# Who forms the lower parts of W_out's blocks in the first MLP of an attention-and-two-MLPs kernel: VectorE instead of GpSimd

## The chip, the cores and the metric

The kernel runs on one core of one Trainium2 chip. The core has a matrix engine (TensorE, PE in the profile; its weight loads are PEld), three engines for elementwise work (VectorE, DVE; ScalarE, ACT; GpSimd, POOL), and a queue that issues the DMAs (SyncE, SP). Each engine takes its instructions strictly in the order of its own queue, and waits on semaphores for the others. The metric is the device time of one execution in microseconds; the median of several executions is compared.

## The reference

```python
attn = causal_softmax(q @ k.T / sqrt(64) + bias(s)) @ v      # 4 batches, 8 heads, 576 positions, 64 wide
x = attn.reshape(2304, 512)
h = x @ w_in1                                                # 512 -> 2048
x = (max(h, 0) + alpha * min(h, 0)) @ w_out1                 # 2048 -> 512
h = x @ w_in2
out = (max(h, 0) ** 2) @ w_out2
```

All of it is wanted to about float32 precision. The four weight matrices arrive as 64-bit floats.

## The kernel before

The program has three stages in a row: attention (to about 217 us), the first MLP (about 217 to 635 us), and the second MLP, which uses a seven-product scheme in place of eight block products (from 635 us). The change lies in the first MLP.

TensorE multiplies in a format with fewer mantissa bits than float32 (fp32r), so every operand is split into a high part (a cast by ScalarE) and a low part (the operand less its high part), and each product is made as three products: high by high, high by low, low by high (TERMS).

The first MLP runs over three thirds of the tokens (c = 0, 1, 2; 768 tokens each) and, in each, over the 16 blocks f of 128 hidden units: 48 steps. A step has these parts:

- split_w(0, f, 0) makes wi_hi (ScalarE, L526) and wi_lo (L528) from a block of W_in, split_w(0, f, 1) makes wo_hi and wo_lo from a block of W_out. Both subtractions stand on L528, for wi on VectorE and for wo on GpSimd. wi has two buffers, wo three.
- mlp_mm (L552): 24 matmuls into two PSUM banks ph, one for each half of the 768 tokens.
- mlp_act: for each half, two VectorE instructions that read ph (L571, L572) form gg; then ScalarE casts gg to the high part of gs (L574) and VectorE subtracts for the low part (L575). L572 also frees its ph bank for the next step's matmuls.
- mlp_out (L673): 24 matmuls of gs and wo into the accumulators po, one step later than mlp_mm.

Beside that, in the gaps, the weights are turned from 64-bit to 32-bit floats. conv does one half of a block: ScalarE scales the two words (L114 into cv_g, L115 into the destination), VectorE forms a mask and shifts (L116, L117, both into cv_t), and GpSimd adds the two as integers (L120). In the first third of the steps the destinations are the blocks wf of the first MLP's own weights, two in a step. From about 338 us on they are blocks wc of the second MLP: there GpSimd also forms sums and differences of blocks (L151 to L154), SP writes the result to DRAM (w1D, from wc), and since wc has one buffer the next L115 waits for that DMA. For W_out of the second MLP the result is split first (whl: L164, L165).

At each change of the third c, the x of the next third is split into xs (L538 on ScalarE, L539 on VectorE).

The order of the instructions on each engine isn't written by hand: the kernel is built with a scheduler that places instructions by its own estimate of their times. A change of engine for one instruction therefore moves others too.

Of the kernel before, what the change touches and what calls it, by code (L numbers as in the profile page):

```python
# [8 lines left out]
F32 = mybir.dt.float32  # L9
# [10 lines left out]
def attention_then_two_mlps(  # L20
# [13 lines left out]
    nc = tc.nc  # L34
# [485 lines left out]
    def split_w(l, f, half):  # L520
        w = wf[l, f]
        nm = ("wi", "wo")[half]
        pool = pools["mp"] if half else pp
        hi = pool.tile([P, 512], F32R, name=nm + "_hi", tag=nm + "_hi", bufs=2 + half)
        lo = pool.tile([P, 512], F32R, name=nm + "_lo", tag=nm + "_lo", bufs=2 + half)
        nc.scalar.copy(hi, w[:, half])  # L526
        eng = nc.vector if half == 0 else nc.gpsimd
        eng.tensor_sub(lo, w[:, half], hi.bitcast(F32))  # L528
        return hi, lo

    W = 2 * HT
# [76 lines left out]
    for g in range(len(units) + LAG + PVLAG):  # L608
# [23 lines left out]
        if live and i == 3:  # L632

            with tc.issue_after(last):
                if cq:
                    w_conv(*cq.pop(0))
                elif n >= NP - 2:
                    first.append(split_w(0, n - NP + 2, 0))
                elif n >= NP - 6:
                    xs.append(make_xk(0, n - NP + 6))  # L640
            if lq:
                w_load(*lq.pop(0))
# [314 lines left out]
    for step, (c, f) in enumerate(steps):  # L957
# [7 lines left out]
        if step > 0 and step + 1 < len(steps):  # L965
            wi = split_w(0, steps[step + 1][1], 0)
        wo = split_w(0, f, 1)
        if step == 0:
            ph = early
# [85 lines left out]
```

## Time and profile before

| | us |
|---|---|
| median of 3 runs | 1009.21 (1007.92 to 1013.36) |
| the profiled execution | 1006.86 |
| its span, first to last instruction | 1005.1 |
| attention | about 217 |
| first MLP | about 418 |
| second MLP | about 370 |

The profile is of one execution. Busy times of an engine say what it did, not what it cost: an engine's idle time matters only where another engine waits for it. TensorE's granted clock was 0.991 of full speed on average, so nearly all matmuls ran at the upper of its two levels.

### The profile page before, as it was taken

How to read it: one execution, taken by the hardware profiler on the slowest of the kernel's cores; microseconds unless marked ns; L12 is line 12 of the kernel's file. 1: busy time of each engine (PE TensorE's matmuls, PEld its weight loads, DVE VectorE, ACT ScalarE, POOL GpSimd, SP SyncE). 2: the span in 40 equal slices, each digit the busy share in tenths (PEclk: the TensorE clock that was granted, in tenths of full speed). 3: DMA queues.
4: the chain of work that ended last, by engine and by line, in shares of the span. 5: the costliest groups of instructions: out<-in, count | busy, mean ns of one | idle time of the engine just before them, and what ended most of it. 6: DMA issues, size and time to landing. Idle time of an engine off the chain costs nothing.

```text
span 1005.1 us, 18047 instructions
## 1 busy us (share of the span) xinstructions
PE 970.0 (97%) x6440; PEld 896.1 (89%) x6440; DVE 810.3 (81%) x1504; ACT 559.7 (56%) x1120; POOL 470.9 (47%) x526
## 2 busy tenths in 40 slices
PE   6899999999999999999999999989999999999998
PEld 5677778778999989989899999889999999999998
DVE  8799889869888898778896777678985889768774
ACT  7798889964444454434544433456453664446442
POOL 7778777645555567675555441234102540034400
PEclk9799999999999999999999999999999999999999
DMA  6666454314434334445373341854677446754274
GB/s 167 167 161 163 119 128 114 73 33 124 127 126 126 104 119 157 158 157 168 125 230 116 116 156 49 323 159 127 221 278 280 125 151 235 267 182 136 90 254 138
DMA packets 105049, 157.05 MB, mean 156 GB/s; under 512 B 31584, under 2 KB 80224, under 8 KB 99584
## 3 DMA queue, kind: packets, MB, share of 16 engines
q1 hardware_dynamic: 104960, 155.91, 49.3%
q8 instruction: 51, 0.84, 0.3%
q14 instruction: 38, 0.31, 0.1%
HBM read 117.00 MB, written 29.88 MB: 146 GB/s over the span
## 4 chain that ended last, share of the span: by engine, by line
PE 56%; DVE 21%; DMA 8%; POOL 7%; ACT 5%; issue 4%; SPq 0%; POOLq 0%; ACTq 0%; DVEq 0%
PE acc L918 15%; PE ph L552 6%; PE po L673 5%; PE b L791 4%; PE a L791 4%; PE c L791 4%; DVE cv_t L117 3%; PE ps_tr L443 3%; DMA w1D<-wc 3%; PE ps_xb L493 2%; DVE gg L571 2%; PE d L791 2%; DVE wi_lo L528 2%; DVE gg L572 2%; PE ps_xa L482 2%
## 5 line engine op out<-in xcount | busy, mean ns | idle before, releaser
L552 PE MATMUL ph<-xs,wi_hi 128*128 128x384 f32 x768 | 199.5, 339 | 7.2 <-DVE gg L572 4.1
L918 PE MATMUL acc<-w2s,th 128*128 128x256 f32 x1512 | 184.7, 283 | 3.3 <-ACT th L707 3.1
L918 PEld LDWEIGHTS acc<-w2s,th 128*128 128x128 f32 x1512 | 183.3, 192 | 4.3 <-ACT th L707 3.5
L673 PE MATMUL po<-gs,wo_hi 128*128 128x512 f32 (+1 forms) x768 | 166.8, 336 | 1.9 <-DVE xT L262 1.4
L552 PEld LDWEIGHTS ph<-xs,wi_hi 128*128 128x128 f32 x768 | 136.7, 189 | 13.8 <-DVE gg L572 6.0
L673 PEld LDWEIGHTS po<-gs,wo_hi 128*128 128x128 f32 x768 | 121.0, 188 | 16.7 <-DVE xT L262 2.1
L552 PE MATMUL ph<-xs,wi_lo 128*128 128x384 f32 x384 | 129.2, 336 | 0.0
L574 ACT CAST gs<-gg 128x768 fp32r<-128x768 f32 (+1 forms) x48 | 39.8, 829 | 139.8 <-DVE gg L572 139.7
L528 POOL TENSOR_TENSOR wo_lo<-wf,wo_hi 128x512 fp32r<-128x512 f32 x48 | 79.9, 1666 | 70.0 <-ACT wo_hi L526 70.0
L707 ACT CAST th<-g 128x768 fp32r<-128x768 f32 x84 | 69.8, 835 | 75.1 <-PE acc L918 57.0
L708 DVE TENSOR_TENSOR th<-g,th 128x768 fp32r<-128x768 f32 x84 | 84.5, 1014 | 23.2 <-ACT th L707 23.2
L673 PE MATMUL po<-gs,wo_lo 128*128 128x256 f32 (+1 forms) x384 | 99.2, 335 | 0.0
L411 POOL TENSOR_SCALAR pr<-pr,rs 128x128 f32<-128x128 f32 (+3 forms) x128 | 73.7, 589 | 42.0 <-DVE rs L408 17.5
L802 POOL TENSOR_TENSOR g<-g 128x384 f32<-128x384 f32 x24 | 21.1, 877 | 154.0 <-ACT g L801 117.1
L708 DVE TENSOR_TENSOR w1h<-w1f,w1h 128x512 fp32r<-128x512 f32 (+1 forms) x96 | 67.9, 720 | 26.5 <-ACT w1h L707 25.8
L575 DVE TENSOR_TENSOR gs<-gg,gs 128x768 fp32r<-128x768 f32 (+1 forms) x48 | 51.8, 1079 | 38.8 <-ACT gs L574 38.8
L398 ACT ACTIVATE pr<-pr,nmax 128x128 f32<-128x128 f32 (+3 forms) x128 | 71.2, 559 | 16.9 <-DVE nmax L386 11.4
L707 ACT CAST w1h<-w1f 128x512 fp32r<-128x512 f32 (+1 forms) x96 | 53.8, 564 | 43.5 <-PE b L791 24.2
L552 PEld LDWEIGHTS ph<-xs,wi_lo 128*128 128x128 f32 x384 | 72.5, 189 | 0.3 <-issue 0.2
L117 DVE SCALAR_TENSOR_TENSOR cv_t<-cv_g,cv_t 128x512 uint32<-128x512 uint32 x64 | 70.8, 1111 | 1.6
L802 POOL TENSOR_TENSOR g<-u 128x384 f32<-128x384 f32 x48 | 49.4, 1030 | 42.4 <-ACT u L801 42.2
L120 POOL TENSOR_TENSOR wc<-cv_t,wc 128x512 uint32<-128x512 uint32 x32 | 43.7, 1373 | 53.5 <-DVE cv_t L117 26.4
(157 smaller groups left out, 2151.9 us busy)
## 6 DMA issues: line engine op xcount, KB each, us to landing
w2s<-w2D SPq DMA_DIRECT2D x42, 1024.0 KB
w1f<-w1D SPq DMA_DIRECT2D x72, 256.0 KB
raw_w<-in_moe_w_in_dram SPq DMA_DIRECT2D x32, 512.0 KB
w2D<-whl SPq DMA_DIRECT2D x16, 896.0 KB
raw_w<-in_moe_w_out_dram SPq DMA_DIRECT2D x24, 512.0 KB
w1D<-wc SPq DMA_DIRECT2D x8, 896.0 KB
QM<-QS SPq DMA_DIRECT2D x15, 288.0 KB
KH<-KS SPq DMA_DIRECT2D x15, 288.0 KB
```

The lines of the kernel that those rows point to most:

```text
L117: nc.vector.scalar_tensor_tensor(t, g.bitcast(U32), 3, t, ALU.logical_shift_left, ALU.bitwise_or)
L398: last = nc.scalar.activation(o, o, AF.Exp, bias=m, scale=-1.0, accum_out=sums[:, h : h + 1])
L411: nc.gpsimd.tensor_scalar(pr[:, :w], pr[:, :w], rs[:, h : h + 1], 1.0, ALU.mult, ALU.mult)
L528: eng.tensor_sub(lo, w[:, half], hi.bitcast(F32))
L552: nc.tensor.matmul(ph[h][:, :HT], ws[a][:, kb * P : (kb + 1) * P], xs[kb][:, bb, h * HT : (h + 1) * HT], start=(cnt == 0), stop=(cnt == 3 ...
L575: sub = nc.vector.tensor_sub(z[:, 1], a, z[:, 0].bitcast(F32))
L673: nc.tensor.matmul(acc, ws[a][:, m * P : (m + 1) * P], gs[:, bb, c_], start=first_ and z == 0, stop=lst and z == 2, skip_group_check=True,)
L707: a = nc.scalar.copy(dst[:, 0], src)
L708: v = nc.vector.tensor_sub(dst[:, 1], src, dst[:, 0].bitcast(F32))
L791: nc.tensor.matmul(pt[:, :HT], hl[:, a, c0 + kb * P : c0 + (kb + 1) * P], xc[i][:, b, kb, :], start=(first and cnt == 0), stop=(cnt == 5), ...
L802: nc.gpsimd.tensor_tensor(dst, r, r, ALU.mult)
L918: nc.tensor.matmul(acc[tb // 2][:, (tb % 2) * 256 : (tb % 2 + 1) * 256], th[:, x, qq, tb * P : (tb + 1) * P], ws[:, y, (2 * q + qq) % 4, : ...
```

## The change

In split_w, the subtraction for W_out's blocks goes to VectorE, as the one for W_in's blocks does already:

```diff
         nc.scalar.copy(hi, w[:, half])
-        eng = nc.vector if half == 0 else nc.gpsimd
-        eng.tensor_sub(lo, w[:, half], hi.bitcast(F32))
+        nc.vector.tensor_sub(lo, w[:, half], hi.bitcast(F32))
         return hi, lo
```

48 instructions leave GpSimd's queue and 48 of the same shape (128 x 512) join VectorE's. From L528 on, each line's number is one lower in the changed file. The scheduler's order moves in these places.

VectorE, one step in the first third of the first MLP, before (cv_t belongs to the conversion of weights, gg and gs to the activation):

```order
L575 TENSOR_TENSOR gs<-gg,gs 128x768
L116 TENSOR_SCALAR cv_t<-cv_g 128x512
L117 SCALAR_TENSOR_TENSOR cv_t<-cv_g,cv_t 128x512
L116 TENSOR_SCALAR cv_t<-cv_g 128x512
L117 SCALAR_TENSOR_TENSOR cv_t<-cv_g,cv_t 128x512
L571 TENSOR_SCALAR gg<-ph,alpha_sb 128x384
L572 SCALAR_TENSOR_TENSOR gg<-ph,gg 128x384
L571 TENSOR_SCALAR gg<-ph,alpha_sb 128x384
```

and now:

```order
L574 TENSOR_TENSOR gs<-gg,gs 128x768
L116 TENSOR_SCALAR cv_t<-cv_g 128x512
L117 SCALAR_TENSOR_TENSOR cv_t<-cv_g,cv_t 128x512
L116 TENSOR_SCALAR cv_t<-cv_g 128x512
L117 SCALAR_TENSOR_TENSOR cv_t<-cv_g,cv_t 128x512
L527 TENSOR_TENSOR wo_lo<-wf,wo_hi 128x512
L570 TENSOR_SCALAR gg<-ph,alpha_sb 128x384
L571 SCALAR_TENSOR_TENSOR gg<-ph,gg 128x384
L570 TENSOR_SCALAR gg<-ph,alpha_sb 128x384
L527 TENSOR_TENSOR wi_lo<-wf,wi_hi 128x512
L571 SCALAR_TENSOR_TENSOR gg<-ph,gg 128x384
```

The wo_lo stands behind the second L117 and ahead of all four instructions of the activation; the rest of the step keeps its order.

VectorE at the start of the first MLP, before:

```order
L571 TENSOR_SCALAR gg<-ph,alpha_sb 128x384
L528 TENSOR_TENSOR wi_lo<-wf,wi_hi 128x512
L116 TENSOR_SCALAR cv_t<-cv_g 128x512
L572 SCALAR_TENSOR_TENSOR gg<-ph,gg 128x384
L117 SCALAR_TENSOR_TENSOR cv_t<-cv_g,cv_t 128x512
L575 TENSOR_TENSOR gs<-gg_first,gs 128x384
L571 TENSOR_SCALAR gg<-ph,alpha_sb 128x384
L575 TENSOR_TENSOR gs<-gg,gs 128x384
```

and now:

```order
L570 TENSOR_SCALAR gg<-ph,alpha_sb 128x384
L527 TENSOR_TENSOR wi_lo<-wf,wi_hi 128x512
L116 TENSOR_SCALAR cv_t<-cv_g 128x512
L571 SCALAR_TENSOR_TENSOR gg<-ph,gg 128x384
L527 TENSOR_TENSOR wo_lo<-wf,wo_hi 128x512
L117 SCALAR_TENSOR_TENSOR cv_t<-cv_g,cv_t 128x512
L574 TENSOR_TENSOR gs<-gg_first,gs 128x384
L570 TENSOR_SCALAR gg<-ph,alpha_sb 128x384
L527 TENSOR_TENSOR wo_lo<-wf,wo_hi 128x512 x2
L574 TENSOR_TENSOR gs<-gg,gs 128x384
```

The first four instructions keep their order; three wo_lo come behind them, ahead of the second half of the first step's gs.

GpSimd in the stretch where it works for the second MLP's W_in, before:

```order
L120 TENSOR_TENSOR wc<-cv_t,wc 128x2x256
L528 TENSOR_TENSOR wo_lo<-wf,wo_hi 128x512
L120 TENSOR_TENSOR wc<-cv_t,wc 128x2x256
L151 TENSOR_TENSOR wc<-wc 128x256
L153 TENSOR_TENSOR wc<-wc 128x256
L152 TENSOR_TENSOR wc<-wc 128x256
L154 TENSOR_TENSOR wc<-wc 128x256
L528 TENSOR_TENSOR wo_lo<-wf,wo_hi 128x512
```

and now, in its last part:

```order
L120 TENSOR_TENSOR wc<-cv_t,wc 128x512
L153 TENSOR_TENSOR wc<-wc 128x256
L120 TENSOR_TENSOR wc<-cv_t,wc 128x2x256
L151 TENSOR_TENSOR wc<-wc 128x256
L152 TENSOR_TENSOR wc<-wc 128x256
L154 TENSOR_TENSOR wc<-wc 128x256
```

The instructions on wc now follow each other with none of another kind between.

## Rows read from the trace of the kernel before

**Rows 1.** The page: busy time of each engine, share of span, instructions.

```profile
PE 970.0 (97%) x6440; PEld 896.1 (89%) x6440; DVE 810.3 (81%) x1504; ACT 559.7 (56%) x1120; POOL 470.9 (47%) x526
```

**Rows 2.** Instructions of L528: shortest, median, longest ns; first and last start.

```profile
L528 DVE TENSOR_TENSOR wi_lo<-wf,wi_hi x48: 680/1222/1743, 202.2 to 607.9; 128x512 fp32r<-128x512 f32 x48
...
L528 POOL TENSOR_TENSOR wo_lo<-wf,wo_hi x48: 1292/1744/2014, 223.8 to 611.9; 128x512 fp32r<-128x512 f32 x48
```

**Rows 3.** Stretches: length, busy PE, PEld, DVE, ACT, POOL; granted clock; DMA.

```profile
217.00:635.00 418.00, 408.89 (x2326) 378.81 (x2325) 343.09 (x457) 191.37 (x309) 219.07 (x170) 1.00 0.41 134
217.00:247.00 30.00, 27.57 (x161) 25.04 (x160) 24.96 (x33) 14.24 (x26) 13.34 (x9) 1.00 0.29 88
247.00:340.00 93.00, 93.00 (x535) 86.56 (x534) 81.96 (x112) 46.17 (x79) 47.84 (x34) 1.00 0.40 125
340.00:505.00 165.00, 159.82 (x896) 147.18 (x894) 137.05 (x178) 72.92 (x116) 105.76 (x86) 0.99 0.43 148
505.00:605.00 100.00, 99.94 (x576) 94.01 (x577) 74.06 (x102) 44.90 (x68) 50.42 (x41) 1.00 0.46 149
```

**Rows 4.** Timeline, VectorE, one step: start us, duration us; idle before, releaser.

```profile
264.20 0.42 DVE L116 TENSOR_SCALAR cv_t<-cv_g 128x512 uint32<-128x512 uint32 x1
264.65 1.67 DVE L117 SCALAR_TENSOR_TENSOR cv_t<-cv_g,cv_t 128x512 uint32<-128x512 uint32 x1
266.25 0.60 DVE L571 TENSOR_SCALAR gg<-ph,alpha_sb 128x384 f32<-128x384 f32 x1
...
267.88 1.38 DVE L528 TENSOR_TENSOR wi_lo<-wf,wi_hi 128x512 fp32r<-128x512 f32 x1
269.19 0.55 DVE L572 SCALAR_TENSOR_TENSOR gg<-ph,gg 128x384 f32<-128x384 f32 x1
270.64 0.96 DVE L575 TENSOR_TENSOR gs<-gg,gs 128x768 fp32r<-128x768 f32 x1 [0.90 <-ACT gs L574]
...
271.97 0.69 DVE L117 SCALAR_TENSOR_TENSOR cv_t<-cv_g,cv_t 128x512 uint32<-128x512 uint32 x1
272.58 0.42 DVE L116 TENSOR_SCALAR cv_t<-cv_g 128x512 uint32<-128x512 uint32 x1
```

**Rows 5.** Timeline, GpSimd, the same step.

```profile
264.43 1.34 POOL L120 TENSOR_TENSOR wf<-cv_t,wf 128x512 uint32<-128x512 uint32 x1 [4.09 <-DVE cv_t L117]
265.73 1.74 POOL L528 TENSOR_TENSOR wo_lo<-wf,wo_hi 128x512 fp32r<-128x512 f32 x1
267.44 1.28 POOL L120 TENSOR_TENSOR wf<-cv_t,wf 128x512 uint32<-128x512 uint32 x1
```

**Rows 6.** Chain of waits, two steps in the last third: start us, us, what.

```profile
519.94 4.16 PE ph L552 x24
...
528.26 4.16 PE ph L552 x24
```

**Rows 7.** Timeline at the start of the first MLP, VectorE, GpSimd and TensorE.

```profile
223.94 1.74 DVE L528 TENSOR_TENSOR wi_lo<-wf,wi_hi 128x512 fp32r<-128x512 f32 x1
225.61 1.48 DVE L116 TENSOR_SCALAR cv_t<-cv_g 128x512 uint32<-128x512 uint32 x1
...
223.84 2.96 POOL L528 TENSOR_TENSOR wo_lo<-wf,wo_hi 128x512 fp32r<-128x512 f32 x2 [7.12 <-ACT wo_hi L526]
...
227.61 0.62 PE L552 MATMUL ph<-xs,wi_hi 128*128 128x384 f32 x2 [2.24 <-DVE gg L572]
```

**Rows 8.** Waits (us in all, times, longest), then timeline, 420 to 447 us.

```profile
ACT wc L115 <- DMA w1D<-wc: 30.3, 8, 5.7
...
421.61 1.31 POOL L528 TENSOR_TENSOR wo_lo<-wf,wo_hi 128x512 fp32r<-128x512 f32 x1
...
432.29 1.22 ACT L115 ACTIVATE wc<-raw_w 128x512 uint32<-128x512 uint32 x2 [5.65 <-DMA w1D<-wc]
...
435.39 0.62 PE L552 MATMUL ph<-xs,wi_hi 128*128 128x384 f32 x2 [0.99 <-DVE gg L572]
...
446.85 0.61 PE L673 MATMUL po<-gs,wo_hi 128*128 128x512 f32 x2 [0.43 <-DVE gs L575]
```

## The prediction, made before the changed kernel was timed

> **What bounds the kernel now.** I read the page's busy times first: TensorE is busy 97% of the span, VectorE 81%, GpSimd 47% [rows 1]. So the question is not who is busiest but where TensorE waits, and for whom. The edit touches only the first MLP, 217 to 635 us, so I then read that stretch in a table of stretches [rows 3]. TensorE is busy 408.89 of 418 us there. All the idle time that any change of the elementwise engines could give back is therefore 9.1 us, under 1% of the run. The table also shows where it lies: 2.4 us in the first 30 us, none between 247 and 340 us, 5.2 us between 340 and 505 us, almost none (0.06 us) between 505 and 605 us, and the remaining 1.4 us at the end.
>
> "None" between 247 and 340 us hides something, which the timeline shows. One step of VectorE runs from 264.20 to 272.58 us, 8.38 us [rows 4]; one step of TensorE where nothing holds it up takes 528.26 - 519.94 = 8.32 us [rows 6]. So in the first third VectorE's own loop, closed by the 0.90 us in which it waits for ScalarE's cast, is longer than TensorE's by 0.06 us a step, and sets the pace. VectorE has no slack there at all: each further microsecond on it lengthens a step, if nothing else gets shorter.
>
> **What gets shorter: VectorE and GpSimd hold each other up.** The same L117 takes 1.67 us at 264.65 and 0.69 us at 271.97 [rows 4]. In the first case GpSimd runs L120 from 264.43 to 265.77 [rows 5], and L117 ends at 266.32, 0.55 us behind that. wi_lo, 680 ns at its shortest [rows 2], takes 1.38 us at 267.88 and ends 0.54 us behind the L120 that ends at 268.72 [rows 4, 5]. So a VectorE instruction with two operands in SBUF gets hardly anything done while GpSimd runs one of these. The other way round too: wo_lo took 1292 ns at its shortest, and 1.74 us where it began beside the unfinished L117 [rows 2, 5]. The instructions that read PSUM (L571, 0.60 us beside wo_lo) aren't touched [rows 4, 5].
>
> **The change, part by part.** It removes 48 instructions from GpSimd (1292 ns or more each) and adds 48 to VectorE. VectorE's price for the same shape is that of wi_lo: 0.68 us alone, and about 0.61 us from one start to the next, since neighbours overlap a little (L117 at 271.97, the next start at 272.58) [rows 2, 4]. If GpSimd got in the way each time it would be 1.31 us, as for wi_lo from 267.88 to 269.19 [rows 4]. The shortest row is the nearest one where GpSimd stands still, the other where it doesn't; 48 of them are 29 to 63 us more on VectorE. It has 418 - 343 = 75 us idle in the stretch, but not in every part of it [rows 3], so I go part by part.
>
> *Start, 217 to 247 us.* TensorE stood 2.24 us for L572 at 227.61 [rows 7]. L572 was late because wi_lo (1.74) and L116 (1.48) ran into two wo_lo on GpSimd, 223.84 to 226.80 [rows 7]. Alone these take 0.68 and 0.42 us [rows 2, 4], so 2.1 us of the wait goes: in the new order nothing was put ahead of L572. But three wo_lo (1.8 us) now stand between it and the second half of the first gs, for which the first mlp_out waits. Carrying the starts on with the short durations, that gs ends at 230.05 us; TensorE, through with 12 matmuls of ph (from 225.5) and the six of mlp_out that need no low part, wants it at 228.75: 1.3 us of the 2.1 are given back. I take 0.8 us of gain for this part; bounds 0 and the 2.4 us that TensorE is idle in it [rows 3].
>
> *First third, 247 to 340 us, 11 steps.* Each step gains a wo_lo behind the second L117. It starts the moment L117 ends, before GpSimd can have been told that cv_t is ready, so it goes first and costs 0.61 us. The second L120 now begins about where wo_lo began before, is held by VectorE's wo_lo until about 266.95, and ends near 268.2. wi_lo starts about 0.6 us later than before, at 268.5, so GpSimd is done and wi_lo costs 0.60 instead of 1.31 us. VectorE's loop becomes 8.38 + 0.61 - 0.71 = 8.28 us, just below TensorE's 8.32, and TensorE sets the pace: 11 x 0.06 = 0.7 us gained. Since wo_lo stands ahead of the activation, the first L572 of a step ends 0.6 us later in its turn than before, and TensorE waits for that instruction; what it has to spare there is used up once, so between 0 and 0.6 us is paid once, and I take 0.3. Sum 0.4 us. The bounds are wide: if wi_lo stays blocked the loop is 8.38 + 0.61 = 8.99 us, 11 x 0.61 = 6.7 us lost; if wo_lo is blocked as well, 11 x 1.31 = 14.4 us.
>
> *340 to 505 us.* Here the chain runs through GpSimd: conversion, four sums, the DMA to w1D, and then ScalarE, which stands 30.3 us in eight waits for that DMA (5.7 us the longest), with its casts of wi and gs queued behind [rows 8]. GpSimd's wo_lo sit inside this chain: the one at 421.61 stood between the two L120 of a block, and pushed the DMA, and with it ScalarE's L115 at 432.29, back by 1.3 us or more. Behind that L115 came wi_hi, wi_lo, L572, and TensorE's 0.99 us at 435.39 [rows 8]. Without it that gap goes, and with it one of the same kind at 446.85 (0.43 us) [rows 8]: 1.4 us. VectorE is idle 28 us of 165 here [rows 3], and 19 wo_lo of 0.61 us are 11.6 us; ScalarE's wo_hi is queued ahead of the waiting L115 in nearly all blocks, so VectorE doesn't take over ScalarE's wait. What is not cured is the change of thirds, where TensorE waits for xs and then for a while runs at the lower of its two clocks (0.99 of full speed over the stretch [rows 3]): xs is held up on ScalarE by the block before it, which begins some 0.4 us earlier, since one wo_lo of 1.3 us leaves GpSimd ahead of it and one of 0.61 us on VectorE, with some blocking, comes in. Together 1.8 us; bounds 0 and 5.2.
>
> *505 to 635 us.* VectorE is idle 26 of 100 us and TensorE hardly at all [rows 3]. 14 wo_lo (8.5 us) fit in. Nothing.
>
> *Second MLP.* It keeps its instructions; its order moves slightly at the start. I take it to shift as a whole; 1 us either way.
>
> Sum: 0.8 + 0.4 + 1.8 = 3.0 us gained. Against the profiled execution (1006.86 us) that gives 1003.9; its own time is 2.35 us below the median of the runs shown, and I take the gain off the median: 1009.2 - 3.0 = **1006.2 us**. A difference of under 0.5% (5 us) is about what a measurement of this kernel can't tell from no change.
>
> **Rivals.**
> 1. *VectorE's loop stays above TensorE's.* The margin in the first third is 0.04 us a step. If GpSimd's L120 starts ahead of wo_lo, or ends after wi_lo has begun, the loop is up to 8.99 us. For it: no slack in those 11 steps; against it: the starts above. It decides from 0.04 us of blocking a step. Price 6.7 us, less 0.8 at the start, with nothing gained later since VectorE then lags there too: 1009.2 + 5.9 = 1015.1 us, slower. The Trainium skill ("SBUF — State Buffer", Who interferes with whom) has a rule on which this rival rests: VectorE with two SBUF inputs and a GpSimd instruction that reads SBUF exclude each other for a whole instruction, and who starts first, not what kind it is, decides who waits. By that rule the rival comes whole or not at all in a step, and 0.1 us in the start of one L120 decides; the trace agrees as far as the 0.54 us left over behind each L120 go.
> 2. *Most of TensorE's idle time closes.* If the shorter chain on GpSimd also frees the change of thirds, and VectorE's relief carries over, 7.7 of the 9.1 us and the 0.7 us of the loop go: 8.4 us, 1000.8. For it: ScalarE's 30.3 us of waiting [rows 8]; against it: xs is formed on VectorE beside the instructions on wc, which stay on GpSimd.
> 3. *Nothing reaches the end.* The second MLP starts with transfers that follow the end of the first; if the moved order there eats the gain, 1009 us.
>
> **How the numbers follow.** Forecast 0.55 (own range 1003 to 1009), rival 1 0.20, rival 2 0.15, rival 3 0.10. Faster by over 0.5% is rival 2 (0.15) and 0.10 of the forecast, where more gaps close than I counted: 0.25. Slower by over 0.5% is three quarters of rival 1: 0.15. The rest, 0.60, is within. The range for 8 in 10 takes in rival 2's time and most of rival 1's: 1000 to 1014.
>
> **What would show it.** Right: no wait of TensorE for L572 at the start but one of about 1 us for gs or wo_lo; steps of 8.32 us in the first third with wi_lo near 0.7 us; ScalarE's wait for the w1D DMA well under 30 us; TensorE's gaps near 435 us gone. Wrong: wi_lo or wo_lo above 1 us in the first third with steps above 8.4 us (rival 1), no gap at the change of thirds (rival 2), or a longer wait for weights at the start of the second MLP (rival 3).

## The result and the profile after

The changed kernel takes 1000.13 us (median of 4 runs, 997.48 to 1002.22); the kernel before, over its 4 runs, 1009.14 us. The ratio is 0.9911, with a 95% interval of 0.9888 to 0.9934: 0.9% faster. The prediction said 1006.2 us and a range of 1000.0 to 1014.0. The time is 0.1 us inside the range, the sign is right, and the gain is three times the 3.0 us that I forecast. The time is where rival 2 had it (1000.8 us).

The profiled execution takes 1000.48 us, its span is 998.7 us: 6.4 us less than the profiled execution of before. The stretch of the first MLP, from TensorE's first ph matmul to the start of the mlp_out behind its last one, as one row of the table of stretches for each kernel (length; busy PE, PEld, DVE, ACT, POOL; granted clock; DMA), before:

```profile
217.19:623.78 406.59, 398.92 (x2271) 370.39 (x2270) 333.67 (x442) 185.71 (x299) 219.07 (x170) 1.00 0.41 135
```

and after:

```profile
216.67:617.57 400.90, 396.57 (x2271) 370.60 (x2270) 329.47 (x491) 187.91 (x299) 147.65 (x122) 1.00 0.42 137
```

5.7 us of the gain lie here, and 0.5 us ahead of it. VectorE has 49 instructions more in the stretch and is busy 4.2 us less. The same table in the first three parts of [rows 3], after:

```profile
217.00:247.00 30.00, 28.99 (x167) 26.14 (x166) 25.24 (x40) 15.88 (x28) 8.55 (x6) 1.00 0.33 104
247.00:340.00 93.00, 93.00 (x539) 87.40 (x538) 81.06 (x126) 46.78 (x78) 35.82 (x26) 1.00 0.40 126
340.00:505.00 165.00, 161.68 (x916) 150.81 (x915) 136.71 (x200) 76.83 (x123) 75.24 (x65) 0.99 0.46 158
```

Set beside the starts of the same matmuls before, TensorE's starts after tell where the time went. TensorE began the MLP 0.5 us earlier (216.67 for 217.19), which is not counted:

| place (times of before) | gained on TensorE, us | forecast |
|---|---|---|
| start, 217 to 253 | 1.3 | 0.8 |
| steps of the first third, 253 to 343 | 0.6 | 0.4 |
| first change of thirds, 343 to 385 | 3.0 | 0.4 of the 1.8 |
| 385 to 432 | 0.0 | |
| around 432 to 455 | -1.6 | 1.4 of the 1.8 |
| 455 to 490 | 0.1 | |
| second change of thirds, 490 to 525 | 2.3 | 0 |
| to 624 | 0.0 | 0 |
| sum | 5.7 | 3.0 |

**The step in the first third.** Timeline of VectorE after, from one L117 to the next one in the same place; it answers to [rows 4]:

```profile
269.21 1.67 DVE L117 SCALAR_TENSOR_TENSOR cv_t<-cv_g,cv_t 128x512 uint32<-128x512 uint32 x1
270.80 0.68 DVE L527 TENSOR_TENSOR wo_lo<-wf,wo_hi 128x512 fp32r<-128x512 f32 x1
...
273.04 0.68 DVE L527 TENSOR_TENSOR wi_lo<-wf,wi_hi 128x512 fp32r<-128x512 f32 x1
...
277.49 1.66 DVE L117 SCALAR_TENSOR_TENSOR cv_t<-cv_g,cv_t 128x512 uint32<-128x512 uint32 x1
```

and of GpSimd in the same step, as [rows 5]:

```profile
268.99 1.34 POOL L120 TENSOR_TENSOR wf<-cv_t,wf 128x512 uint32<-128x512 uint32 x1 [4.63 <-DVE cv_t L117]
271.05 1.59 POOL L120 TENSOR_TENSOR wf<-cv_t,wf 128x512 uint32<-128x512 uint32 x1 [0.72 <-DVE cv_t L117]
```

wo_lo starts when L117 ends and 0.25 us ahead of the second L120, which is held to 1.59 us and ends at 272.64. wi_lo comes 0.40 us behind that, and takes 0.68 us where it took 1.38. The loop is 277.49 - 269.21 = 8.28 us.

**The start.** Timeline after, VectorE, then TensorE, as [rows 7]:

```profile
223.42 0.68 DVE L527 TENSOR_TENSOR wi_lo<-wf,wi_hi 128x512 fp32r<-128x512 f32 x1
224.02 0.42 DVE L116 TENSOR_SCALAR cv_t<-cv_g 128x512 uint32<-128x512 uint32 x1
...
227.02 1.87 DVE L527 TENSOR_TENSOR wo_lo<-wf,wo_hi 128x512 fp32r<-128x512 f32 x2
228.81 0.55 DVE L574 TENSOR_TENSOR gs<-gg,gs 128x384 fp32r<-128x384 f32 x1
...
229.41 0.62 PE L672 MATMUL po<-gs,wo_hi 128*128 128x512 f32 x2 [0.90 <-DVE gs L574]
```

The wait of 2.24 us is gone, and one of 0.90 us for gs has come.

**A lead that the table of stretches doesn't show.** How far does VectorE run ahead of TensorE? The 15th subtraction for gs (the first step has two, so it is that of the 14th step) and the mlp_out that needs it, before:

```profile
337.72 0.96 DVE L575 TENSOR_TENSOR gs<-gg,gs 128x768 fp32r<-128x768 f32 x1 [0.90 <-ACT gs L574]
...
339.07 0.51 PE L673 MATMUL po<-gs,wo_hi 128*128 128x512 f32 x2
```

and after:

```profile
333.01 0.96 DVE L574 TENSOR_TENSOR gs<-gg,gs 128x768 fp32r<-128x768 f32 x1 [0.90 <-ACT gs L573]
...
336.65 0.51 PE L672 MATMUL po<-gs,wo_hi 128*128 128x512 f32 x2
```

Before, the gs starts 1.35 us ahead, and in each step from the fifth to this one it is 1.34 to 1.37 us. After, it is 2.0 us at 243 us, 3.2 us at 259 us, and grows by 0.05 us a step to 3.6 us. So VectorE was 4.7 us earlier at the end of the third, and TensorE only 2.4 us (both with the 0.5 us by which the MLP began earlier). At the change of thirds the other 2.3 us count: ScalarE's casts for xs (L538, L537 after) begin 4.7 us earlier, before

```profile
350.91 2.29 ACT L538 CAST xs<-xT 128x768 fp32r<-128x768 f32 x3
```

and after

```profile
346.24 2.30 ACT L537 CAST xs<-xT 128x768 fp32r<-128x768 f32 x3
```

and TensorE's three waits for xs (0.55, 1.16 and 0.61 us) become one of 0.61 us for xs and one of 0.39 us for gg. The first of the three, before:

```profile
352.77 0.45 PE L552 MATMUL ph<-xs,wi_hi 128*128 128x384 f32 x1 [0.55 <-DVE xs L539]
```

and the two after:

```profile
351.48 0.45 PE L551 MATMUL ph<-xs,wi_hi 128*128 128x384 f32 x1 [0.61 <-DVE xs L538]
...
361.56 0.62 PE L551 MATMUL ph<-xs,wi_hi 128*128 128x384 f32 x2 [0.39 <-DVE gg L571]
```

**The lower clock.** Timeline of TensorE before, from the second of those waits on:

```profile
354.73 0.44 PE L552 MATMUL ph<-xs,wi_hi 128*128 128x384 f32 x1 [1.16 <-DVE xs L539]
...
356.14 0.69 PE L552 MATMUL ph<-xs,wi_hi 128*128 128x384 f32 x1 [0.61 <-DVE xs L539]
...
356.94 1.16 PE L552 MATMUL ph<-xs,wi_hi 128*128 128x384 f32 x3
```

The table of stretches there, before:

```profile
355.00:360.00 5.00, 4.39 (x16) 4.07 (x16) 5.00 (x6) 1.93 (x3) 4.92 (x5) 0.66 0.00 1
```

and the same stretch after:

```profile
355.00:360.00 5.00, 5.00 (x28) 4.34 (x27) 4.97 (x11) 1.74 (x4) 1.00 (x1) 1.00 0.45 184
```

Before, the granted clock is 0.66 on average over these 5 us: nine matmuls from 356.14 to 359.19 us run at the lower level (1.2 GHz) and take 3.05 us, where 24 take 4.16 us at the upper one [rows 6], so nine would take 1.56. That is 1.5 us that every table counts as busy. After, the clock stays at 1.00.

**What got worse.** After, around 439 us: ScalarE, VectorE and TensorE in the timeline:

```profile
435.92 0.66 ACT L115 ACTIVATE wc<-raw_w 128x512 uint32<-128x512 uint32 x1 [7.77 <-DMA w1D<-wc]
...
437.12 1.35 DVE L527 TENSOR_TENSOR wi_lo<-wf,wi_hi 128x512 fp32r<-128x512 f32 x1 [3.95 <-ACT wi_hi L526]
...
438.99 0.62 PE L551 MATMUL ph<-xs,wi_hi 128*128 128x384 f32 x2 [2.23 <-DVE gg L571]
```

and the stretch behind, with its granted clock of 0.66:

```profile
440.00:445.00 5.00, 5.00 (x21) 4.62 (x20) 4.93 (x9) 2.08 (x4) 2.85 (x3) 0.66 0.34 105
```

The two waits of [rows 8] became one of 2.23 us, with a spell of its own at the lower clock. ScalarE's waits for the w1D transfer are as long as before (us in all, times, longest):

```profile
ACT wc L115 <- DMA w1D<-wc: 30.9, 8, 7.8
```

### The profile page after: what moved, and what is told of

It reads as the page before. It is cut to its first block, busy times and chain, and to the rows that moved or that the text cites. A ratio compares the mean times of both kernels' runs of the same rounds, so it can differ in the third digit from the quotient of the medians.

```text
span 998.7 us, 18060 instructions
## 1 busy us (share of the span) xinstructions
PE 970.2 (97%) x6440; PEld 899.7 (90%) x6440; DVE 806.6 (81%) x1552; ACT 561.9 (56%) x1120; POOL 401.5 (40%) x478
## 4 chain that ended last, share of the span: by engine, by line
PE 68%; DVE 14%; DMA 6%; POOL 4%; ACT 4%; issue 4%; SPq 0%; DVEq 0%; POOLq 0%; ACTq 0%
PE acc L917 15%; PE ph L551 11%; PE po L672 10%; PE b L790 4%; PE a L790 4%; PE c L790 4%; PE ps_tr L443 3%; PE ps_xb L493 3%; PE d L790 2%; PE ps_xa L482 2%; DMA w1D<-wc 2%; PE ps_sc L357 2%; DVE gg L570 2%; PE ps_sc L358 2%; POOL wc L120 2%
## 5 line engine op out<-in xcount | busy, mean ns | idle before, releaser
L551 PE MATMUL ph<-xs,wi_hi 128*128 128x384 f32 x768 | 197.0, 336 | 3.4 <-DVE gg L571 2.6
L120 POOL TENSOR_TENSOR wc<-cv_t,wc 128x512 uint32<-128x512 uint32 x32 | 48.0, 1506 | 144.0 <-DVE cv_t L117 111.1
L574 DVE TENSOR_TENSOR gs<-gg,gs 128x768 fp32r<-128x768 f32 (+1 forms) x48 | 48.1, 1002 | 37.4 <-ACT gs L573 37.4
L120 POOL TENSOR_TENSOR wf<-cv_t,wf 128x512 uint32<-128x512 uint32 x32 | 45.8, 1431 | 74.0 <-DVE cv_t L117 71.9
L570 DVE TENSOR_SCALAR gg<-ph,alpha_sb 128x384 f32<-128x384 f32 x95 | 57.9, 609 | 13.8 <-PE ph L551 13.5
```

Of the source, the lines that this page charges most:

```text
L120: nc.gpsimd.tensor_tensor(d, t, d, ALU.add)
L551: nc.tensor.matmul(ph[h][:, :HT], ws[a][:, kb * P : (kb + 1) * P], xs[kb][:, bb, h * HT : (h + 1) * HT], start=(cnt == 0), stop=(cnt == 3 ...
L570: nc.vector.tensor_scalar(x, ph[h][:, :HT], 0.0, alpha_sb[:, f : f + 1], ALU.min, ALU.mult)
L574: sub = nc.vector.tensor_sub(z[:, 1], a, z[:, 0].bitcast(F32))
```

## The experiments

The lead in the table below is that of the 15th gs over its mlp_out, as above; "xs waits" are TensorE's waits for xs at the first change of thirds; "stretch" is the first MLP as above, from the one execution of each kernel that was profiled; the clock is the granted one from 355 to 360 us, with the first three steps moved from 353 to 358 us.

| kernel | median us | stretch us | lead us | xs waits us | clock behind them |
|---|---|---|---|---|---|
| before | 1008.24 to 1009.14 | 406.59 | 1.35 | 2.32 | 0.66 |
| wo_lo moved in the later thirds | 1005.50 | 405.30 | 1.34 | 2.32 | 0.66 |
| own tile for L115, in before | 1005.52 | 402.83 | 1.35 | 2.06 | 0.66 |
| moved from the fourth step on, first third | 1006.04 | 404.42 | 2.26 | 1.73 | 1.00 |
| moved in the first three steps | 1001.56 | 403.12 | 2.57 | 1.73 | 0.66 |
| moved in the first third | 999.48 | 401.24 | 3.60 | 0.62 | 1.00 |
| changed kernel | 1000.13 | 400.90 | 3.64 | 0.61 | 1.00 |
| changed kernel, own tile for L115 | 994.04 | 395.57 | 3.68 | none | 1.00 |

My theory after the comparison (A): the gain comes from the first third, where GpSimd's silence gives VectorE a lead that is cashed at the change of thirds. The rival (B): it comes from GpSimd's shorter chain beside the conversion of the second MLP's weights, where the prediction looked for most of it. Each edit also lets the scheduler place other instructions anew; no run holds the order fixed.

### The first third alone

The engine becomes a parameter of split_w (the kernel before, with the lines between left out):

```diff
-    def split_w(l, f, half):
+    def split_w(l, f, half, eng=nc.vector):
...
-        eng = nc.vector if half == 0 else nc.gpsimd
...
-        wo = split_w(0, f, 1)
+        wo = split_w(0, f, 1, nc.vector if c == 0 else nc.gpsimd)
```

> wo_lo on VectorE in the 16 steps of the first third only; in the other 32 steps GpSimd keeps it. Theory A (the gain is made in the first third: 1.3 us at the start and 0.6 us in the steps on TensorE, and a lead of VectorE over TensorE, which at the change of thirds makes the w1D transfer and with it xs earlier, so that TensorE waits 1.0 us there where it waited 2.3 us, and its spell at the lower clock, 1.5 us, doesn't come): TensorE's instructions run 4.9 us earlier than in the kernel before from about 385 us on, the waits between 430 and 455 us are those of the kernel before, and the end is 4.9 us earlier: 1004.2 us. Theory B (GpSimd's shorter chain beside the conversion of the second MLP's weights makes it): only the start and the steps of the first third gain, 1.9 us: 1007.2 us, and the spell at the lower clock near 356 us is there.

999.48 us, ratio 0.9906 (0.9893 to 0.9919): all of the gain, and the stretch is 5.35 us shorter. The clock doesn't fall near 356 us. Theory A forecast 4.9 us in the stretch and stands; B's 1.9 us is out. The 8.8 us in the median are more than either forecast; in the profiled execution 2.4 us of what exceeds the stretch lie behind it (see below, on the medians). A was wrong in one thing: the waits between 430 and 455 us weren't those of before, they were gone, and one of 1.01 us came at 471 us. ScalarE's waits for w1D are shorter by a third, though GpSimd's chain there is that of before:

```profile
ACT wc L115 <- DMA w1D<-wc: 20.7, 7, 4.4
```

That the conversion's chain, with its other place in time, met the other engines elsewhere is my reading of this; no run isolates it.

### The later thirds alone

```diff
...
-        wo = split_w(0, f, 1)
+        wo = split_w(0, f, 1, nc.vector if c > 0 else nc.gpsimd)
```

> The complement: wo_lo stays on GpSimd in the first third, and goes to VectorE in the 32 steps behind it. Theory A: the start and the first change of thirds are those of the kernel before (a wait of 2.2 us near 227 us, three waits near 353 to 356 us, the lower clock for some 3 us behind them); behind that the changed kernel's part, which cost 1.6 us near 439 us and gained 2.3 us between 490 and 525 us: 0.7 us faster, 1008.4 us. Theory B: the rest of the gain, 6.2 - 1.9 = 4.3 us: 1004.8 us.

1005.50 us, ratio 0.9960 (0.9945 to 0.9974); the stretch is 1.3 us shorter. The first change of thirds is that of before, with the spell at the lower clock. By the places of the table above, TensorE loses 1.2 us between 385 and 455 us, and gains 2.3 us between 490 and 525 us, as much as the changed kernel does there: the waits of 0.60 and 0.36 us are gone. In the stretch this is A's account (0.7 us forecast, 1.3 measured). The time of the whole is less clear: 2.8 us by the medians, and 0.9945 to 0.9974 is 2.6 to 5.5 us, which leaves out A's 0.7 and takes in B's 4.3. The profiled execution took 1000.95 us, the fastest of six by 3.8 us, and 4.0 us of what it gained lie behind the stretch, where neither theory had anything. The two halves of the change give 8.8 and 2.8 us in the medians, and the whole 9.0, so they don't add up: on top of the first third the second half brings nothing to be seen in the medians, and 0.3 us in the stretch (401.24 to 400.90 us). The whole has the wait at 439 us and the lower clock behind it, which the first third alone doesn't have.

### GpSimd does the work a second time

```diff
         nc.vector.tensor_sub(lo, w[:, half], hi.bitcast(F32))
+        if half == 1:
+            ghost = pool.tile([P, 512], F32R, name="ghost", tag="ghost", bufs=1)
+            nc.gpsimd.tensor_sub(ghost, w[:, half], hi.bitcast(F32))
```

> The changed kernel, and GpSimd forms each wo_lo a second time, into a tile that nothing reads: VectorE's work is that of the changed kernel, GpSimd's is that of the kernel before. Theory A (VectorE pays for wo_lo with what GpSimd's silence gives back): the loop of VectorE in the first third is 8.38 + 0.61 = 8.99 us or more, 11 x 0.67 = 7.4 us lost there, and the gain at the start and at the change of thirds is gone: 1009.1 + 7.4 = 1016.5 us or more. The rival (what counts is that wo_lo no longer waits in GpSimd's queue and that the order on VectorE is another; GpSimd's silence is worth little): within 2 us of the changed kernel, 998 to 1002 us.

1028.34 us, ratio 1.0194 (1.0181 to 1.0207). Timeline of one step, VectorE, GpSimd, again VectorE, TensorE:

```profile
287.77 1.78 DVE L527 TENSOR_TENSOR wo_lo<-wf,wo_hi 128x512 fp32r<-128x512 f32 x1
...
287.25 1.74 POOL L530 TENSOR_TENSOR ghost<-wf,wo_hi 128x512 fp32r<-128x512 f32 x1
288.96 1.72 POOL L120 TENSOR_TENSOR wf<-cv_t,wf 128x512 uint32<-128x512 uint32 x1
...
291.11 0.68 DVE L527 TENSOR_TENSOR wi_lo<-wf,wi_hi 128x512 fp32r<-128x512 f32 x1
...
290.72 0.45 PE L554 MATMUL ph<-xs,wi_hi 128*128 128x384 f32 x1 [0.78 <-DVE gg L574]
```

The ghost starts 0.5 us ahead of wo_lo, and wo_lo ends 0.56 us behind it: 1.78 us, not 0.68. VectorE's loop is 9.38 us, 1.1 us more than after, which is what wo_lo takes longer (wi_lo takes 0.68 us in both), and from 272 us on TensorE waits 0.77 us or more in each step of the third. So moving wo_lo pays because GpSimd falls silent, not because wo_lo is out of GpSimd's queue. Theory A gave the sign and a lower bound (1016.5 us); it took wo_lo to run free and the loop at 8.99 us.

By the Trainium skill ("SBUF — State Buffer", Who interferes with whom) a VectorE instruction with two SBUF inputs and a GpSimd instruction that reads SBUF exclude each other, and the order of issue decides who waits. The trace agrees both ways: wo_lo gives way to the ghost (1.78 us), and the L120 behind the ghost gives way to wo_lo (1.72 us, where the L120 that comes first, at 268.99 after, takes 1.34).

### The first three steps, and the rest of the first third

```diff
...
-        wo = split_w(0, f, 1)
+        wo = split_w(0, f, 1, nc.vector if step < 3 else nc.gpsimd)
```

> wo_lo on VectorE in the first three steps only. Theory A in its stronger form (the lead that VectorE wins at the start, some 1.9 us over TensorE at 262 us, is kept through the first third although VectorE's loop is 8.38 us again, because a loop 0.06 us longer than TensorE's eats only 0.7 us of it in 11 steps): TensorE steps of 8.32 us up to 340 us, VectorE's subtraction for gs still 2.5 us or more earlier than in the kernel before at 337 us, and 2 to 3 us gained at the change of thirds: 1009.1 - 1.3 - 0.6 - 2.4 = 1004.8 us. Theory A in its weaker form (the lead comes from the shorter loop, step by step): steps of 8.38 us and nothing at the change of thirds: 1009.1 - 1.3 = 1007.8 us.

1001.56 us, ratio 0.9927 (0.9915 to 0.9939): three instructions moved out of 48 give three quarters of the gain by the medians, and 3.5 of 5.7 us in the stretch (A forecast 4.3 us; the median is 3.2 us below its 1004.8). VectorE's loop is 8.38 us as before, but its lead is 3.2 us at 252 us and shrinks by 0.07 us a step to 2.57 us, and TensorE meanwhile runs steps of 8.32 us. That is the stronger form of A; of the 2 to 3 us at the change of thirds, only 1.2 us came, and the lower clock came there too. The timeline of TensorE:

```profile
352.54 0.44 PE L551 MATMUL ph<-xs,wi_hi 128*128 128x384 f32 x1 [1.11 <-DVE xs L538]
353.95 0.57 PE L551 MATMUL ph<-xs,wi_hi 128*128 128x384 f32 x1 [0.62 <-DVE xs L538]
```

and the stretch, granted clock 0.66:

```profile
353.00:358.00 5.00, 4.38 (x16) 4.07 (x16) 5.00 (x6) 1.92 (x3) 4.92 (x5) 0.66 0.05 19
```

The complement within the third:

```diff
...
-        wo = split_w(0, f, 1)
+        wo = split_w(0, f, 1, nc.vector if 3 <= step < 16 else nc.gpsimd)
```

> wo_lo on VectorE from the fourth to the sixteenth step only; the first three steps and the 32 steps of the other thirds leave it on GpSimd. Theory A (a lead of VectorE over TensorE that is won in the first three steps, and only kept by the shorter loop, makes the gain at the change of thirds): the start is that of the kernel before, with TensorE's wait of 2.2 us near 227 us; the subtraction for gs runs 1.4 us ahead of the mlp_out that needs it, and that grows by 0.05 us a step to about 2.0 us; 0.6 us gained in the steps and 0.5 us at the change of thirds, where the lower clock is still seen: 1.1 us below the kernel before, about 1007.2 us. The rival (the lead grows wherever GpSimd is silent, and the later stretches gain whatever the start did): 0.6 us in the steps, 2.5 us at the change of thirds, 2.1 us behind it: 1003.1 us.

1006.04 us, ratio 0.9970 (0.9953 to 0.9987). The lead starts at 1.45 us, jumps to 1.8 us in the first moved step and grows by 0.04 us a step to 2.26 us, and the stretch is 2.2 us shorter: more than A's 1.1, far from the rival's 5.2. The profiled execution was the slowest of twelve (1008.99 us). A's lower clock did not come, though the waits are those of the kernel above (timeline of TensorE, then the stretch behind):

```profile
355.63 0.44 PE L551 MATMUL ph<-xs,wi_hi 128*128 128x384 f32 x1 [1.12 <-DVE xs L538]
357.04 0.44 PE L551 MATMUL ph<-xs,wi_hi 128*128 128x384 f32 x1 [0.61 <-DVE xs L538]
```

```profile
360.00:365.00 5.00, 4.47 (x24) 3.63 (x23) 4.93 (x7) 1.20 (x3) 2.56 (x3) 1.00 0.45 184
```

### What is left: ScalarE behind the w1D transfer

In the conversion of the second MLP's blocks, L115 gets a tile of its own, and GpSimd's L120 writes wc:

```diff
-        nc.scalar.activation(d, low, AF.Copy, scale=2.0**-29)
+        r = d
+        if len(dst.shape) == 3:
+            r = pools["prep"].tile([P, 2, 256], U32, name="cv_l", tag="cv_l", bufs=2)
+        nc.scalar.activation(r, low, AF.Copy, scale=2.0**-29)
...
-        nc.gpsimd.tensor_tensor(d, t, d, ALU.add)
+        nc.gpsimd.tensor_tensor(d, t, r, ALU.add)
```

> The changed kernel, and for blocks of the second MLP ScalarE's L115 writes into a tile of its own, which GpSimd's L120 then adds to cv_t into wc; so it is GpSimd that waits for the w1D transfer, and no more ScalarE with its casts behind the wait. Theory C (what TensorE still waits for behind 340 us is ScalarE's queue behind that transfer): ScalarE's waits for w1D, 30.9 us, are gone, and with them TensorE's wait of 2.23 us at 439 us, its spell at the lower clock behind it (1.9 us), and the waits of 0.61 and 0.39 us at the change of thirds: 5 us below the changed kernel, 995 us. Rival D: the L120 that waits keeps cv_t, VectorE's next L116 waits for that buffer, and the same wait comes back through VectorE's queue: within 1 us of the changed kernel, 999 to 1001 us, or above.

994.04 us, ratio to before 0.9865 (0.9839 to 0.9891): the fastest here, and 1 us from theory C's 995. The stretch is 395.57 us, 5.3 below the changed kernel. ScalarE has no wait for w1D any more; GpSimd has it, and TensorE keeps two waits between 217 and 612 us, 0.90 us at the start and one at the change of thirds. The wait (us in all, times, longest), then TensorE's timeline:

```profile
POOL wc L123 <- DMA w1D<-wc: 24.6, 5, 5.6
```

```profile
357.72 0.62 PE L554 MATMUL ph<-xs,wi_hi 128*128 128x384 f32 x2 [0.55 <-DVE gg L574]
```

The same edit in the kernel before:

> The same edit in the kernel before, with wo_lo on GpSimd. Theory C: the waits at the change of thirds (2.3 us) and the lower clock behind them (1.5 us) go, and the waits near 435 and 447 us (2.5 us with the restarts); the start and the loop of 8.38 us stay: 6.3 us below the kernel before, 1002 us. Rival D: the wait moves to GpSimd, with wo_lo queued behind it, and TensorE then waits for wo_lo: no gain, 1008 us or above.

1005.52 us, ratio 0.9971 (0.9957 to 0.9985): 3.6 us, not C's 6.3. The waits near 435 and 447 us went as forecast, those for xs did not, and the clock fell behind them (timeline of TensorE, then the stretch):

```profile
352.96 0.44 PE L555 MATMUL ph<-xs,wi_hi 128*128 128x384 f32 x1 [0.90 <-DVE xs L542]
354.91 0.44 PE L555 MATMUL ph<-xs,wi_hi 128*128 128x384 f32 x1 [1.16 <-DVE xs L542]
```

```profile
355.00:360.00 5.00, 5.00 (x20) 4.82 (x20) 4.96 (x6) 2.50 (x4) 4.92 (x5) 0.66 0.00 0
```

TensorE gained nothing at this change of thirds (0.0 us). This separates two things that the trace of before had mixed. With ScalarE free and VectorE's lead at 1.35 us, xs is late all the same; with ScalarE free and a lead of 3.68 us it isn't late at all. At the first change of thirds the lead decides.

With the first third moved only, and the tile:

> wo_lo on VectorE in the first third only, and the tile of its own for L115. Theory C: the six waits that were left behind 340 us with the first third alone (0.62, 0.51, 0.38, 1.01, 0.57 and 0.39 us) go: 3.5 us below that kernel's 999.5, 996.0 us. Rival D: GpSimd has both the wait for w1D and, in the later thirds, the wo_lo behind it, so TensorE waits for wo_lo: above 999.5 us.

997.28 us, ratio 0.9888 (0.9865 to 0.9912): 2.2 us below the first third alone, between C (996.0) and D; the stretch is 397.01 us, 4.2 us below (C: 3.5). Without ScalarE's wait the later thirds' wo_lo seem worth moving after all: 1.4 us in the stretch, and 3.2 us by the medians (997.28 to 994.04), whose intervals overlap.

### The 0.90 us at the start

On top of the fastest kernel, the wo_lo of the second and third step each go behind the gs of the step before (the second step's at 228.51 us, the third step's at 234.55 us):

```diff
-        wo = split_w(0, f, 1)
+        if step in (1, 2):
+            with tc.issue_after(anchor_v):
+                wo = split_w(0, f, 1)
+        else:
+            wo = split_w(0, f, 1)
```

> The changed kernel with the tile of its own for L115, and the wo_lo of the second and third step placed behind the first step's gs on VectorE, where two of them stood ahead of it. Theory (the 0.90 us that TensorE still waits near 229.5 us is the price of those two wo_lo): that wait goes, everything else stays as with the tile alone: 0.9 us below its 994.0, 993.1 us, with VectorE's lead over TensorE at 250 us not smaller than 2.6 us. Rival: the moved wo_lo then stand ahead of the conversion and the next activation, VectorE's lead falls and the wait comes back there: 994 us or above.

994.95 us, no gain. The wait near 229.5 us went, and TensorE was 1.2 us earlier at 340 us than without the edit. But VectorE's lead was 2.0 us at 251 us and 2.93 at the end of the third (3.68 without), and 1.0 of the 1.2 us was paid back at the change of thirds, where these waits stand in place of the one of 0.55 us:

```profile
350.13 0.45 PE L554 MATMUL ph<-xs,wi_hi 128*128 128x384 f32 x1 [0.39 <-DVE xs L541]
357.70 0.61 PE L554 MATMUL ph<-xs,wi_hi 128*128 128x384 f32 x2 [0.84 <-DVE gg L574]
```

The stretch is 395.37 us, 0.2 shorter. The rival had it: a wait of TensorE closed at the price of VectorE's lead is no gain.

### Why the medians differ by more than the profiles

The kernel before once more, unchanged:

> The kernel before, unchanged, for a second profile: how much of the 3.3 us by which the medians differ more (9.0 us) than TensorE's first-MLP stretch in the two profiles (5.7 us) lies in this stretch. If the stretch is a property of the kernel, it is within 0.5 us of 406.6 us again, with waits at the same places, and the 3.3 us lie in the attention and the second MLP; if the spell at the lower clock near 356 us varies from one execution to the next, the stretch differs by up to 1.5 us.

1008.07 us; the stretch is 405.93 us, and the clock from 355 to 360 us is 0.66 again. The waits are at the same places but for two: that of 0.60 us near 494 us isn't there, which makes most of the 0.66 us between the two, and one of 0.39 us is at 432 us. So the stretch, to 0.7 us, and the spell belong to the kernel.

Behind the stretch this execution takes 383.6 us and the first one 381.3: TensorE waited 4.97 us for the second MLP's first weights where it had waited 3.77, and ran longer at the lower clock behind that. The table of stretches, the first execution and then this one:

```profile
640.00:670.00 30.00, 26.23 (x142) 25.65 (x142) 19.51 (x32) 16.21 (x32) 11.58 (x13) 0.94 0.76 283
640.00:670.00 30.00, 25.03 (x129) 24.66 (x128) 17.86 (x31) 14.97 (x31) 10.76 (x13) 0.89 0.70 265
```

The granted clock from 640 to 670 us tells most of what the profiled executions above, the ghost's left out, differ by behind the stretch: 377.3 to 379.5 us where it is 1.00 (the later thirds, the first three steps, the first third, and the changed kernel with the tile), 381.0 and 381.3 us where it is 0.94, 380.4 to 383.6 us where it is 0.89 (the changed kernel, 381.1 us, among them). So some 6 us lie between the shortest and the longest of them where no wo_lo is made. The first third alone held the upper clock there, and its mean granted clock was 0.995 to 0.997 in all five executions (changed kernel: 0.989 to 0.992); its median probably owes part of its 8.8 us to that.

The first profile of before (1006.86 us) was 2.3 us under the median, and that is most of what the medians (9.0 us) show beyond the profiles (6.4 us). Why the wait for the second MLP's first weights varies from one execution to the next stays open.

## Why the prediction was right or wrong

**"All the idle time that could be given back is 9.1 us."** Wrong as a bound; the sum didn't use it, rival 2 and the bounds of the parts did. The nine matmuls at the lower clock counted as busy: 1.5 us more. The prediction named the lower clock and gave it no price.

**Start, 0.8 us.** The mechanism was right: the 2.24 us wait went, and gs became late behind the wo_lo. Its size was 1.3 us, since the new wait was 0.90 us, not 1.3.

**First third, 0.4 us.** Right: VectorE's loop was forecast at 8.28 us and measured 8.28, with wi_lo at 0.68 and wo_lo ahead of the second L120; 0.6 us gained. The one-off 0.3 us was not seen. Rival 1 didn't come, and the ghost shows that its mechanism is real: with GpSimd busy ahead of wo_lo the loop was 9.38 us. The margin was wider than the 0.1 us that the prediction gave: wo_lo was 0.25 us ahead of the L120.

**340 to 505 us, 1.8 us: the step that failed, twice.** The sum was made from TensorE's waits in each part, as if a part began where the one before had left it. It took the block ahead of xs to begin 0.4 us earlier; it began 4.7 us earlier, 2.0 more than the matmuls that need xs (349.13 for 351.78). The relief of VectorE at the start, a lead of 3.2 us where it had 1.35, was counted only as far as TensorE waited there, and the rest was dropped; the change of thirds cashed it, 3.0 us with the clock. The other half, that GpSimd's chain to w1D would shorten ScalarE's wait and close the gaps near 435 and 447 us, was wrong: the wait stayed (30.3 and 30.9 us), and a longer gap came, 1.6 us the other way. Moving the chain earlier doesn't shorten a wait when the waiting instruction is earlier too. Nor do the wo_lo in GpSimd's chain set its length: with the first third alone moved they stayed there, and the wait was 20.7 us.

**505 to 635 us, nothing.** The second change of thirds (490 to 525 us) gained 2.3 us, part of it behind 505 us: waits of 0.60 and 0.36 us and the restarts behind them are gone. The later thirds alone gave the same 2.3 us there, so this gain comes from their own wo_lo and not from the first third. VectorE's lead is the likely cause here too: in the 31st and 32nd step it is 1.7 and 0.6 us before, 5.4 and 3.0 us after, 4.4 and 2.7 us with the later thirds alone. Part of it, 0.7 us, also came in the second execution of the kernel before, which didn't have the wait of 0.60 us.

**The chances.** Rival 2 was near the outcome in its time, and in "VectorE's relief carries over"; its other half, the shorter chain on GpSimd, did not come. Against it the prediction held that xs is formed beside GpSimd's work on wc; that stayed true (L538's subtractions for xs still take up to 1.5 us), and the earlier start outweighed it. At 0.15 it was put too low. That the time lies in the range is in part luck: the lower end was set at 1000 us to take in rival 2, and the forecast's own range, 1003 to 1009 us, missed by 2.9 us; and the two errors of the 340 to 505 us part, 2.6 us too little at the change of thirds and 3.0 us too much around 440 us, nearly cancel there.

## What to carry to other kernels

Where two engines hold each other up, moving work from the less busy to the busier one can make the busier one faster: price the move by what the other engine's silence gives back, as the 0.68 and 1.78 us of the same instruction show. When a stretch is relieved, write down not only the waits of the last engine but also how far its supplier runs ahead of it, because that lead is kept through steps that look balanced and is spent at the next irregular place. And where the granted clock fell behind a wait, count the time at the lower clock as part of that wait's price: a table of busy times doesn't show it.

## What the runs showed of the hardware that I had not expected

TensorE's clock does not follow from the waits alone. After waits of 1.11 and 0.62 us it fell (0.66 from 353 to 358 us, the first three steps moved), after 1.12 and 0.61 us it stayed at 1.00 (moved from the fourth step on). After one wait of 2.23 us it fell to 0.66 (changed kernel, 440 to 445 us); after one of 2.26 us, with the later thirds moved, it did not (timeline, then the stretch):

```profile
444.81 0.62 PE L551 MATMUL ph<-xs,wi_hi 128*128 128x384 f32 x2 [2.26 <-DVE gg L571]
```

```profile
445.00:450.00 5.00, 5.00 (x29) 4.64 (x29) 4.27 (x8) 2.79 (x5) 2.10 (x2) 1.00 0.35 116
```

The wait of 2.24 us at the start of before left it at 1.00 too [rows 3, rows 7]. Within one kernel it repeated (before, two profiles). So a wait of about 2 us may cost 1.5 us more or nothing; what decides it these runs don't tell.
